# Router logits on four column tiles, copied back through another PSUM bank, and the routes of an attention-and-MoE kernel dealt to other tile steps

## The chip, the cores and the metric

The kernel runs on one core of a Trainium2 chip. The metric is the device time of one execution in microseconds, as the median of several runs. The five engines of the core have their own instruction queues, worked off in order: TensorE (PE in the profile; PEld are its weight loads), VectorE (DVE), ScalarE (ACT), GpSimd (POOL) and SyncE (SP, which here only issues DMAs).

## What is computed

Two stages, in float32. The first is a linear attention with a decaying state over 4 batches, 8 heads, 768 tokens and a head size of 48:

```python
for t in range(S):
    cur = np.einsum('bhd,bhe->bhde', u[None] * kt, vt)
    y[:, :, t] = np.einsum('bhd,bhde->bhe', rt, state + cur)
    state = w[None, :, :, None] * state + np.einsum('bhd,bhe->bhde', kt, vt)
```

The second is a mixture of experts on the 3072 token rows of 384 numbers that come out of it. A token with a positive skip score goes to the expert with its largest gate logit (8 experts, hidden size 1024), the others pass through:

```python
do_compute = x @ w_skip > 0
logits = xc @ w_gate
e_idx = np.argmax(logits, axis=1)
gate_w = probs[np.arange(len(xc)), e_idx]
y[mask] = gate_w[mask, None] * (np.maximum(xc[mask] @ w1[e], 0.0) @ w2[e])
out[do_compute] = xc + y
```

## The kernel before

**Tiles.** The tokens are cut into 24 tiles: 2 pairs of batches, 12 steps of 64 tokens, and a tile holds one step of both batches of a pair. The loop `for n in range(NT - 1)` (L905) is software-pipelined: in step n TensorE makes for tile n+1 the scores (`scores`, L441), the product with the old state (`across`, L527), for tile n+2 the transposed keys (`turn_k`, L454), for tile n the transposed output rows (`turn_x`, L569), then the new state of tile n+1 (`state`, L474) and the masked scores times values (`within`, L503). VectorE masks the scores (L462, L463) between `scores` and `within`, and prepares tile n+3 (`prep_r`, L411 and L419); GpSimd scales its keys (`prep_k`, L429) and makes half of the split of an expert weight (L114); ScalarE copies out of PSUM (`kt` L456, `xT` L572, `sblk` L483, `xt` L538) and makes the other parts of the preparation (L405, L113). `within` has an added dependence on ScalarE's copy of kt of tile n+2 (or of xT, where there is none). SP loads tile n+5, its values, and one of the first 24 weight pieces a step, and stores two output transfers for each tile (three for tiles 12 to 15).

There are 8 PSUM banks: ps_p and ps_y two each, ps_s, ps_r, ps_t, ps_l one each. Work of two engines on one bank is put in order by the builder.

**Logits.** After every fourth tile (`n % GB == GB - 1`) `gate_some` (L593) multiplies the transposed rows of four tiles with the gate and skip weights (9 columns for each of two batches, spread over a stationary side of 64 columns): 3 chunks x 2 halves = 6 matmuls of 256 moving columns into two column tiles of ps_l. ScalarE copies them to `lt` (L606). One step later `gate_back` (L608) turns them back to tokens on partitions with two matmuls against `pick` (a sum of identity columns) into the free columns of ps_t, behind the 384 columns that `turn_x` uses, and ScalarE copies them to `lg` (L621). For tiles 20 to 22 this happens at the end of the loop, and tile 23 has its own `gate` (L576).

**Routes.** `route(g0, g1)` (L634) is a generator that finds for a group of tiles each token's expert, its rank in that expert's list (with matmuls of the one-hot choice against a triangle and against ones, in ps_r), and writes token number and weight into the lists by a matmul of one-hot lanes (`ol`, L778 or L737) with values (`vl`, L789 or L744), the collect (L796 or L750). It yields a kind: 0 is VectorE work that `tick(k)` may run next, up to k pieces a step; 1, 2 and 4 mark TensorE work, run at one fixed place of a step behind `turn_x` (from step 20 on also at its end). The groups are tiles 0 to 7, 8 to 15, 16 to 19 and 20 to 23. A group can start as soon as its last logits are back. `tick` gets (1, 1, 2)[n % 3] pieces below step 16, 3 below step 20 and 6 from there on. With the group that ends at tile 15, the first gather of rows (for the first tile of expert 0, L122 on GpSimd) is issued. The first three groups run in the loop, the last behind it.

**Behind the loop** (L949 to L982) the first expert's first 128 rows are worked in pieces, `run(k)`, between the end of the attention: turn the rows, `turn_x(23)`, `gate_back` for tiles 20 to 22, three matmuls of the expert (L194), `gate(23)`, the score part of the last route, six matmuls, its rank matmuls, and so on. Then come the experts.

Of the kernel before, what the change touches and what calls it, by code (L numbers as in the profile page):

```python
# [9 lines left out]
F32 = mybir.dt.float32  # L10
F32R = mybir.dt.float32r
# [43 lines left out]
FIRST = 12  # L55
GROUPS = [(0, 8), (8, 16), (16, 20), (20, 24)]
# [3 lines left out]
def tile_wkv_moe(  # L60
# [183 lines left out]
    with ExitStack() as actx:  # L244
# [45 lines left out]
        wgp = tab.tile([P, NCC, 2, C], F32, name="wgp")  # L290
        nc.sync.dma_start(out=wgp, in_=wgq)
        pick = tab.tile([P, NB, E + 1], F32, name="pick")
# [77 lines left out]
        def setup_routes():  # L370
            nc.vector.memset(before, 0.0)
            rows = ident.rearrange("p (c q e) -> p c q e", c=2, q=NB)[:, :, :, : E + 1]
# [189 lines left out]
        gts, xcopy = {}, {}  # L562
        seen = [-1]

        def turn_x(n):
# [4 lines left out]
            if n % GB == 0:  # L570
                gts[0] = wk.tile([P, NCC, 2, GB, C], F32, tag="xT", name=f"xT{n}", bufs=1)
            xcopy[n] = nc.scalar.copy(  # L572
                gts[0][:, :, :, n % GB, :], pt[:, :DM].rearrange("p (j c t) -> p j c t", j=NCC, c=2)
            ).ins

        def gate(n):  # L576
            half = slice(n % 2 * C, (n % 2 + 1) * C)
            pg = ps_y[half, 0, DM : DM + NB * (E + 1)]
            for j in range(NCC):
                for c in range(2):  # L580
                    nc.tensor.matmul(
                        pg,
                        gts[0][:, j, c, n % GB, :],
# [9 lines left out]
        def gate_some(n, k=GB):  # L593
            pg = ps_l[:, : k * C]
            for j in range(NCC):
                for c in range(2):
                    nc.tensor.matmul(  # L597
                        pg[c * C : (c + 1) * C, :],
                        wgp[:, j, c, :],
                        gts[0][:, j, c, :k, :].rearrange("p k t -> p (k t)"),  # L600
                        start=(j == 0),
                        stop=(j == NCC - 1),
                        skip_group_check=True,
                    )
            lt = turned_lg[n] = wk.tile([P, GB * C], F32, tag="lt", name=f"lt{n}", bufs=1)[:, : k * C]
            nc.scalar.copy(lt, pg)  # L606

        def gate_back(n, k=GB):  # L608
            lt = turned_lg.pop(n)
            w = NB * (E + 1)  # L610
            for j in range(0, k, 2):
                m = min(2, k - j) * C
                nc.tensor.matmul(
                    ps_t[:m, DM + j // 2 * w : DM + (j // 2 + 1) * w],
                    lt[:, j * C : j * C + m],
                    pick.rearrange("p q e -> p (q e)"),
                    start=True,
                    stop=True,
                )
            g0, full = n - k + 1, k // 2 * 2  # L620
            nc.scalar.copy(  # L621
                lg[:, g0 : g0 + full, :].rearrange("p n e -> p (n e)"), ps_t[:, DM : DM + full // 2 * w]
            )
# [712 lines left out]
```

## Time and profile before

| | |
|---|---|
| median of 3 runs | 274.98 us (274.95 to 278.34) |
| profiled execution, its own time | 276.32 us |
| its span, first to last instruction | 274.2 us |
| busy share of the span | PE 93%, PEld 85%, DVE 67%, ACT 51%, POOL 48% |
| granted TensorE clock | 0.998 of full |
| moved by DMA | 54.30 MB, mean 198 GB/s |

A line of the profile gives start and length in us, engine, line of the kernel, operation and the tiles written and read, with xN for N merged instructions; in brackets stands the idle time before it and what ended it. A line of groups gives the busy time of all N and the mean of one in ns, then idle time and releasers. The chain is the sequence of work that ended last, each piece with what it waited for. fp32 matmuls appear as two records each.

### The profile page before, as it was taken

The page shows a single profiled execution, that of the slowest core. Times are in us where ns is not written, and L with a number is a line of the kernel's source. Part 1 is how long each engine was busy: PE and PEld are TensorE (multiplying, and loading weights), DVE is VectorE, ACT ScalarE, POOL GpSimd, SP SyncE. Part 2 cuts the span into 40 slices and gives each one's busy share as a digit, 9 for nine tenths or more (in the row PEclk, how much of TensorE's full clock was granted, in tenths as well). Part 3 has the DMA queues.
Part 4 walks back from the last instruction along what each step waited for, and adds up shares of the span by engine and source line. Part 5 has one row for each costly group of instructions (what it writes and reads, how often), then busy time and mean ns, then how long its engine had stood idle before and what let it go on. Part 6 is the DMA issues. An engine that isn't in the chain of part 4 may idle for free.

```text
span 274.2 us, 8740 instructions
## 1 busy us (share of the span) xinstructions
PE 255.6 (93%) x3545; PEld 233.9 (85%) x3545; DVE 183.2 (67%) x372; ACT 141.1 (51%) x316; POOL 131.4 (48%) x131
## 2 busy tenths in 40 slices
PE   7998999999979989788999999999999999999990
PEld 2797897878869877776879999999999999999990
DVE  8786657598896899954655686757748377483310
ACT  2664566667756756434455554717548085480300
POOL 8536313375545538511748853763525535255011
PEclk9999999999999999999999999999999999999999
DMA  7977678878999995435479994694837747100010
GB/s 201 308 197 240 163 203 277 248 247 256 289 274 282 272 284 159 114 93 143 111 254 308 365 379 166 219 317 145 260 121 241 241 142 261 43 4 27 15 35 23
DMA packets 31140, 54.30 MB, mean 198 GB/s; under 512 B 4535, under 2 KB 14412, under 8 KB 31088
## 3 DMA queue, kind: packets, MB, share of 16 engines
q1 hardware_dynamic: 28896, 48.19, 57.2%
q0 software_dynamic: 2048, 5.44, 5.8%
q8 instruction: 30, 0.49, 0.7%
q14 instruction: 22, 0.18, 0.2%
q10 hardware_dynamic: 144, 0.00, 0.0%
HBM read 45.82 MB, written 8.65 MB: 199 GB/s over the span
## 4 chain that ended last, share of the span: by engine, by line
PE 82%; DVE 10%; ACT 3%; issue 2%; DMA 1%; POOL 0%; POOLq 0%; ACTq 0%
PE ps_p L164 11%; PE ps_y L164 11%; PE ps_p L441 8%; PE ps_p L154 5%; PE ps_r L154 5%; PE ps_l L154 5%; PE ps_y L154 5%; PE ps_s L474 5%; PE ps_y L503 5%; PE ps_l L454 4%; PE ps_y L527 3%; PE ps_l L597 3%; PE ps_t L569 3%; PE ps_y L216 2%; PE ps_p L216 2%
## 5 line engine op out<-in xcount | busy, mean ns | idle before, releaser
L114 POOL TENSOR_TENSOR lo<-raw,hi 128x512 fp32r<-128x512 f32 x42 | 57.0, 1358 | 75.3 <-ACT hi L113 55.7
L113 ACT CAST hi<-raw 128x512 fp32r<-128x512 f32 x96 | 55.1, 624 | 0.0
L114 DVE TENSOR_TENSOR lo<-raw,hi 128x512 fp32r<-128x512 f32 x54 | 44.0, 837 | 2.6 <-ACT hi L113 2.3
L429 POOL TENSOR_TENSOR kd<-dm,w_d 128x512 f32<-128x512 f32 x22 | 30.1, 1366 | 14.7 <-DMA dm<-in_dm_dram 13.0
L172 POOL DMA_INDIRECT out_dram<-xg,sid x16 | 17.1, 1067 | 36.4 <-DVE xg L169 25.7
L462 DVE COPY_PREDICATED am<-below,ps_p 128x512 f32<-128x512 int8 x24 | 17.7, 739 | 17.1 <-PE ps_p L441 17.0
L441 PE MATMUL ps_p<-rd,kd 64*64 64x128 f32 x768 | 26.9, 276 | 0.3 <-issue 0.3
L441 PEld LDWEIGHTS ps_p<-rd,kd 64*64 64x64 f32 x768 | 20.9, 132 | 3.2 <-issue 0.7
L158 ACT ACTIVATE hh<-ps_p 128x464 fp32r<-128x464 f32 x7 | 3.9, 559 | 36.9 <-PE ps_p L154 20.1
L122 POOL DMA_INDIRECT xg<-out_dram,gid x16 | 18.2, 1139 | 8.7 <-DVE gw L694 4.0
L503 PE MATMUL ps_y<-vz,am 128*64 128x96 f32 x384 | 20.2, 247 | 2.1 <-DVE am L463 1.5
L503 PEld LDWEIGHTS ps_y<-vz,am 128*64 128x64 f32 x384 | 17.8, 137 | 3.4 <-issue 1.9
L405 ACT ACTIVATE rd<-rd,uw 128x128 f32<-128x128 f32 x52 | 17.8, 395 | 4.9 <-DVE rd L411 4.9
L474 PE MATMUL ps_s<-vz,kt 128*64 128x96 f32 x352 | 19.6, 253 | 0.0
L456 ACT COPY kt<-ps_l 128x512 f32<-128x512 f32 x22 | 12.8, 583 | 12.9 <-PE ps_l L454 12.9
L164 PE MATMUL ps_p<-hi,hh 128*128 128x384 f32 x56 | 19.4, 347 | 0.0
L164 PE MATMUL ps_y<-hi,hh 128*104 128x384 f32 x56 | 18.9, 338 | 0.0
L164 PE MATMUL ps_p<-hi,hl 128*128 128x384 f32 x56 | 18.9, 337 | 0.0
L164 PE MATMUL ps_y<-lo,hh 128*104 128x384 f32 x56 | 18.9, 337 | 0.0
L164 PE MATMUL ps_y<-hi,hl 128*104 128x384 f32 x56 | 18.9, 337 | 0.0
L164 PE MATMUL ps_p<-lo,hh 128*128 128x384 f32 x56 | 18.8, 336 | 0.0
L169 DVE SCALAR_TENSOR_TENSOR xg<-ps_y,gate_s,xg 104x384 f32<-104x384 f32 (+1 forms) x8 | 4.9, 616 | 20.5 <-PE ps_y L164 17.9
(244 smaller groups left out, 693.4 us busy)
## 6 DMA issues: line engine op xcount, KB each, us to landing
raw<-in_w_dram SPq DMA_DIRECT2D x96, 256.0 KB
dm<-in_dm_dram SPq DMA_DIRECT2D x24, 512.0 KB
vz<-in_tok_dram SPq DMA_DIRECT2D x48, 96.0 KB
out_dram<-xt SPq DMA_DIRECT2D x48, 96.0 KB
out_dram<-xt SPq DMA_DIRECT2D x4, 192.0 KB
xg<-out_dram,gid POOLq DMA_INDIRECT x16
out_dram<-xg,sid POOLq DMA_INDIRECT x16
wgp<-in_wgq_dram SPq DMA_DIRECT2D x1, 192.0 KB
```

The lines of the kernel that those rows point to most:

```text
L113: nc.scalar.copy(hi, t)
L114: eng.tensor_tensor(lo, t, hi.bitcast(F32), ALU.subtract)
L122: ins = nc.gpsimd.indirect_dma_start(out=xg, out_offset=None, in_=out[0:rows], in_offset=bass.IndirectOffsetOnAxis(ap=gid[:, q : q + 1], a ...
L154: nc.tensor.matmul(ph, a[:, c, fs], b[:, c, :], start=(k == 0), stop=(k == 3 * NCC - 1))
L164: nc.tensor.matmul(py, a, b[:, f, :], start=(k == 0), stop=(k == 3 * NFC - 1))
L172: ins = nc.gpsimd.indirect_dma_start(out=out, out_offset=bass.IndirectOffsetOnAxis(ap=sid[:, q : q + 1], axis=0), in_=xs.pop(q), in_offset ...
L405: nc.scalar.mul(rd[:, :, 1], rd[:, :, 0], uw[:, hp : hp + 1])
L429: (eng or nc.gpsimd).tensor_tensor(kds[n], d[:, 1], w_d[:, n % NSUB, 1][:, :, None].to_broadcast([DR, NHP, 2, C]), ALU.mult,)
L441: nc.tensor.matmul(ps_p[q * C : (q + 1) * C, a, 2 * hp * C : 2 * (hp + 1) * C], kd[h, hp, q, :], rd[h, hp, q].rearrange("p s c -> p (s c)" ...
L462: nc.vector.copy_predicated(shape(am[n % 2]), below, p[:, :, 0])
L474: nc.tensor.matmul(s[a * C : (a + 1) * C, :, hp * D : (hp + 1) * D], kt[:, hp, a, :], t[:, :, a, hp, :], start=i == 0 and hp == 0, stop=Tr ...
L503: ins = nc.tensor.matmul(place_y(a, c)[:, :, g, :], am[n % 2][:, a, hp * C : (hp + 1) * C], t[:, :, a, hp, :], start=g == 0 and n % NSTEP ...
```

## The change

- `gate_some` cuts its stationary side to 32 columns and its moving side into two halves of 128 columns (two tiles each): 12 matmuls into four column tiles of ps_l. `lt` is 128 columns wide. In the loop it is issued behind `within` and `evac` of the step, except in step 22, where it stays ahead of `within`. The call for tiles 20 to 22 takes all four places of `xT4`, the fourth with old data that nothing reads.
- `gate_back` is one matmul, with a `pick` twice as wide, into the last 36 columns of ps_r in place of ps_t.
- The transposed rows of four tiles lie in one fixed tile, `xT4`.
- The gate weights are half as large (96 KB in place of 192) and are loaded behind the loads of tile 4 in place of ahead of them.
- `tick` takes its number of pieces from the table `DEAL`; in a route of tiles 0 to 15, `ol` is a piece of its own behind `oj`. The steps at the end of steps 20 to 22 are gone. By the table the first route runs in steps 8 to 16 (its `ol` and `vl` in step 15, its collect in step 16), the second in steps 16 to 21 (`ol` and `vl` in step 20, its collect, and with it the first gather, in step 21).
- The route of tiles 16 to 19 (`mid`) no longer runs in steps 20 to 22: its score part, with the weights, runs on VectorE in step 22 behind `gate_some`, its rank matmuls, ranks, `ol` and `vl` behind the loop after `gate_back` of tiles 20 to 22, and one collect of all three values behind `gate(23)`.

```diff
+DEAL = {8: 2, 9: 2, 10: 1, 11: 1, 12: 1, 13: 1, 15: 2, 16: 4, 17: 2, 19: 2, 20: 2}
...
-        wgp = tab.tile([P, NCC, 2, C], F32, name="wgp")
-        nc.sync.dma_start(out=wgp, in_=wgq)
-        pick = tab.tile([P, NB, E + 1], F32, name="pick")
+        wgp = tab.tile([P, NCC, 2, C // 2], F32, name="wgp")
+        pick = tab.tile([P, 2, NB, E + 1], F32, name="pick")
...
         def gate_some(n, k=GB):
-            pg = ps_l[:, : k * C]
+            pg = ps_l[:, : 2 * C]
+            w = C // 2
             for j in range(NCC):
                 for c in range(2):
-                    nc.tensor.matmul(
-                        pg[c * C : (c + 1) * C, :],
-                        wgp[:, j, c, :],
-                        gts[0][:, j, c, :k, :].rearrange("p k t -> p (k t)"),
...
+                    for i in range(2):
+                        nc.tensor.matmul(
+                            pg[(2 * c + i) * w : (2 * c + i + 1) * w, :],
+                            wgp[:, j, c, :],
+                            xT4[:, j, c, 2 * i : 2 * i + 2, :].rearrange("p k t -> p (k t)"),
...
         def gate_back(n, k=GB):
             lt = turned_lg.pop(n)
             w = NB * (E + 1)
-            for j in range(0, k, 2):
-                m = min(2, k - j) * C
-                nc.tensor.matmul(
-                    ps_t[:m, DM + j // 2 * w : DM + (j // 2 + 1) * w],
-                    lt[:, j * C : j * C + m],
-                    pick.rearrange("p q e -> p (q e)"),
...
+            pb = ps_r[:, 512 - 2 * w :]
+            nc.tensor.matmul(pb, lt, pick.rearrange("p s q e -> p (s q e)"), start=True, stop=True)
             g0, full = n - k + 1, k // 2 * 2
-            nc.scalar.copy(
-                lg[:, g0 : g0 + full, :].rearrange("p n e -> p (n e)"), ps_t[:, DM : DM + full // 2 * w]
-            )
+            nc.scalar.copy(lg[:, g0 : g0 + full, :].rearrange("p n e -> p (n e)"), pb[:, : full // 2 * w])
...
         def route(g0, g1):
-            n, late = g1 - g0, g0 >= EARLY
+            n, late, mid = g1 - g0, g0 >= EARLY, EARLY <= g0 and g1 < NT
...
+            if mid:
+                weigh()
+                part_weight()
+                count()
             yield 4 if late else 1
...
                 value(0)
+                if mid:
+                    value(1, 2)
+                    nc.vector.tensor_tensor(before, before, sums, ALU.add)
+                    nc.vector.tensor_scalar(over[:, g0:g1], r1, float(CAP), None, ALU.is_ge)
+                    yield 4
+                    collect(0, NV3)
+                    return
...
-            nc.vector.tensor_tensor(
-                ol, lane[:, None, :].to_broadcast([P, n, P]), lo.unsqueeze(2).to_broadcast([P, n, P]), ALU.is_equal
-            )
             oj = small("oj", w=NSL)
...
             nc.vector.tensor_tensor(before, before, sums, ALU.add)
+            yield 0
+            nc.vector.tensor_tensor(
+                ol, lane[:, None, :].to_broadcast([P, n, P]), lo.unsqueeze(2).to_broadcast([P, n, P]), ALU.is_equal
+            )
             yield 0
...
         load_v(4)
+        nc.sync.dma_start(out=wgp, in_=wgq)
...
-            tick((1, 1, 2)[n % 3] if n < EARLY else 3 if n < TE else 6)
+            tick(DEAL.get(n, 0))
...
+            if n == NT - 2:
+                gate_some(n, NT - 1 - TE)
+                while next(mid) == 0:
+                    pass
+            within(n + 1, kcopy.get(n + 2, xcopy[n]))
+            evac(n + 1)
             if n < TE and n % GB == GB - 1:
                 gate_some(n)
-            elif n == NT - 2:
-                gate_some(n, NT - 1 - TE)
-            within(n + 1, kcopy.get(n + 2, xcopy[n]))
-            evac(n + 1)
             if back:
                 back()
-            if n >= TE:
-                for kind in (1, 2, 4):
-                    step_route(kind)
-                tick()
...
         gate_back(NT - 2, NT - 1 - TE)
+        while next(mid) == 0:
+            pass
         run(1)
         gate(NT - 1)
-        last = route(ends[NT], NT)
+        both(mid)
+        last = route(*GROUPS[3])
```

More of the change, by code (lines that the diff above doesn't have):

```diff
@@ L371, in setup_routes @@
             nc.vector.memset(before, 0.0)
-            rows = ident.rearrange("p (c q e) -> p c q e", c=2, q=NB)[:, :, :, : E + 1]
+            rows = ident.rearrange("p (c s q e) -> p c s q e", c=2, s=2, q=NB)[:, :, :, :, : E + 1]
             nc.vector.tensor_tensor(pick, rows[:, 0], rows[:, 1], ALU.add)
@@ L560, in put_x @@
                 x_out.append(ins.ins)
-        gts, xcopy = {}, {}
+        xT4 = tab.tile([P, NCC, 2, GB, C], F32, name="xT4")
+        xcopy = {}
         seen = [-1]
@@ L569, in turn_x @@
                 nc.tensor.transpose(pt[:, c * P : (c + 1) * P], x[:, c * P : (c + 1) * P], ident)
[L570 to L571 removed]
             xcopy[n] = nc.scalar.copy(
[L573 removed]
+                xT4[:, :, :, n % GB, :], pt[:, :DM].rearrange("p (j c t) -> p j c t", j=NCC, c=2)
             ).ins
@@ L662, in route @@
             yield 0
-            if not late:
+            if not late or mid:
                 nc.scalar.activation(df, df, AF.Exp)
@@ L670, in route, with weigh, part_weight, count @@
             nc.vector.tensor_tensor(oh, eq[:, :, :E], bc(m2), ALU.is_equal)
+            gw = small("gw")
+            gh, gl = small("gh", F32R), small("gl", F32R)
+            sums = sm.tile([P, E], F32, tag="sums", name=f"sums{g0}")
+            def weigh():
+                nc.vector.tensor_reduce(gw, df, AX.X, ALU.add)
+                nc.vector.tensor_scalar(gw, gw, 1e-9, None, ALU.add)
+            def part_weight():
+                nc.vector.reciprocal(gw, gw)
+                nc.vector.tensor_copy(gh, gw)
+                nc.vector.tensor_tensor(gl, gw, gh.bitcast(F32), ALU.subtract)
+            def count():
+                nc.vector.tensor_reduce(sums, oh.rearrange("p n e -> p e n"), AX.X, ALU.add)
+            if mid:
+                weigh()
+                part_weight()
+                count()
             yield 4 if late else 1
@@ L690, in route @@
                 )
-            gw = small("gw")
-            def weigh():
-                nc.vector.tensor_reduce(gw, df, AX.X, ALU.add)
-                nc.vector.tensor_scalar(gw, gw, 1e-9, None, ALU.add)
-            if late:
+            if late and not mid:
                 nc.scalar.activation(df, df, AF.Exp)
-            else:
+            elif not late:
                 weigh()
@@ L702, in route @@
             rk = small("rkp", w=E)
-            gh, gl = small("gh", F32R), small("gl", F32R)
             r1 = small("r1")
-            sums = sm.tile([P, E], F32, tag="sums", name=f"sums{g0}")
             def ranks():
                 nc.vector.tensor_tensor(rk, pr[:, : n * E].rearrange("p (n e) -> p n e", e=E), oh, ALU.mult)
-            def count():
-                nc.vector.tensor_reduce(sums, oh.rearrange("p n e -> p e n"), AX.X, ALU.add)
             if late:
@@ L819, in place @@
             nc.vector.tensor_tensor(gate_s[:, c], lists[:, 1, j], lists[:, 2, j], ALU.add)
-        ends = {g1: g0 for g0, g1 in GROUPS}
+        ends = {g1: g0 for g0, g1 in GROUPS if g1 <= EARLY}
+        mid = route(*GROUPS[2])
         routes = []
@@ L948, in tile_wkv_moe @@
                 piece(n - FIRST_LOAD)
+        assert not routes
         done = NT - 1 - FIRST_LOAD - LEAD
```

32 lines of the change are left out of this document (11 added, 21 removed).

## The prediction, made before the changed kernel ran

> **What bounds the kernel now.** I read the page's head and its chain first, then the chain of waits step by step, then the groups, then the engine timelines of VectorE and TensorE where the chain leaves TensorE.
>
> ```profile
> span 274.2 us, 8740 instructions
> DMA  7977678878999995435479994694837747100010
> PE 82%; DVE 10%; ACT 3%; issue 2%; DMA 1%; POOL 0%; POOLq 0%; ACTq 0%
> ```
>
> 82% of the chain is TensorE; the 10% of VectorE stand at a few places of the attention, which ends shortly before 124.98 us, where the first expert's matmuls begin (a row of part 4). The experts behind it are nearly one run of TensorE, and the change doesn't touch them. So I count what the change does to TensorE's time up to the end of the last attention tile, and then in the bridge to the experts. One undisturbed tile step on the chain:
>
> ```profile
> 35.41 1.03 PE ps_p L441 x32
> 36.44 0.45 PE ps_y L527 x32
> 36.89 0.59 PE ps_l L454 x4
> 37.48 0.33 PE ps_t L569 x3
> 37.81 0.81 PE ps_s L474 x16
> 38.62 0.66 PE ps_y L503 x16
> ```
>
> Scores, across, turn_k, turn_x, state, within: 3.87 us with no gap. Everything a step has above 3.87 is what the change can win.
>
> **Part 1, logits on four column tiles.** Now a call of gate_some is 6 fp32 matmuls (12 records) of 256 columns on two column tiles; then 12 matmuls (24 records) of 128 columns on four.
>
> ```profile
> L597 PE MATMUL ps_l<-xT,wgp 128*64 128x256 f32 x60 | 7.5, 382 | 0.0
> L597 PEld LDWEIGHTS ps_l<-xT,wgp 128*64 128x64 f32 x72 | 5.1, 136 | 2.2 <-ACT xT L572 0.8
> L441 PE MATMUL ps_p<-rd,kd 64*64 64x128 f32 x768 | 26.9, 276 | 0.3 <-issue 0.3
> ```
>
> Five calls take 7.5 us: 1.5 us each, 125 ns a record on two tiles. No record here has a 128x32 tile. The nearest is L441: four tiles at once, 128 columns, 26.9 / 768 = 35 ns a record, and its one change of tile shape per call is in that rate. 24 x 35 ns = 0.84 us. Bounds: if the records scale with columns and tiles alone, 125 / 4 = 31 ns, 0.75 us; if only two of four tiles run at a time, 62.5 ns, 1.5 us and no gain. I take 0.84: saving 0.66 x 5 = 3.3 us. The sixth call (three tiles, 192 columns, by its columns about 1.1 us now; afterwards the same as the others) saves 0.3. Sum **-3.6 us** (-4.1 to +0.4).
>
> The order changes too: state, within and the old gate all use 128x64 tiles, the new gate doesn't, so one more change of shape comes in. The quoted step shows what that may cost: the 16 records of state, behind 128x128 work, take 0.81 us, the same 16 of within, behind state, 0.66: 0.15 us, less than the spread of my bounds. The Trainium skill (TensorEngine Tiling (Array Packing), Key Properties) says against this change that switching the tiling mode, not merely the tile, drains TensorE; it names no price. With 0.15 us a call from the rows above the sum would be 0.75 us less over five calls; I hold it to be in L441's rate already. The same page gives up to 4x for a stationary side of 32 columns, which no run here shows yet.
>
> Putting the gate behind within and evac costs nothing: ScalarE's copy of the logits comes behind the tile's evacuation, ahead of the next turn_k by scores and across (1.48 us); without that cover turn_k would wait for a copy that is smaller than kt's 0.59 us. Loading the weights of the gate (half as large) behind tile 4's loads puts its issue (0.33 us of SP, below) from ahead of tile 4's load to behind the first tile's two output transfers and tile 4's, and ahead of tile 5's load; the first call that reads it comes three steps later, and tile 5 is needed a step later than tile 4.
>
> ```profile
> 9.19 0.33 SPq L291 DMA_DIRECT2D wgp<-in_wgq_dram  x1
> ```
>
> **Part 2, brought back into another bank.** Every fourth step, turn_x writes ps_t, where gate_back has just left logits for ScalarE:
>
> ```profile
> 32.04 0.60 PE ps_l L454 x4
> 32.66 0.59 ACT kt L456
> 33.39 0.55 PE ps_t L569 x3
> PE ps_t L569 <- ACT lg L621: 2.1, 5, 0.5
> L613 PE MATMUL ps_t<-pick,lt 128*128 128x18 f32 x20 | 2.6, 244 | 0.0
> ```
>
> From 32.64 to 33.94 for what takes 0.33 in the quiet step: 0.97 us lost, five times. The transposes start where the lg copy ends, which sits behind the kt copy. With the logits in ps_r that wait has no object; what stays is one matmul in place of two, at most 2.6 / 5 / 2 = 0.26 us. Saving 0.71 x 5 = **-3.6 us** (-4.8 if even the matmul hides in the queue, -1.3 if the wait stays for another reason and only matmuls go). But ps_r is the bank of the routes: at step 16 the collect of the first route, now at step 15, comes right behind gate_back and waits for the same copy, **+0.2 us**.
>
> **Part 3, the table of steps.** VectorE per tile step:
>
> ```profile
> L462 DVE COPY_PREDICATED am<-below,ps_p 128x512 f32<-128x512 int8 x24 | 17.7, 739 | 17.1 <-PE ps_p L441 17.0
> L463 DVE COPY_PREDICATED am<-eye,ps_p 128x512 f32<-128x512 int8 x24 | 17.7, 736 | 0.9
> L411 DVE TENSOR_TENSOR rd<-dm,w_d 128x512 f32<-128x512 f32 x24 | 18.2, 759 | 0.0
> L419 DVE TENSOR_TENSOR rd<-rd,uw 128x256 f32<-128x256 f32 x22 | 13.5, 614 | 0.6
> L778 DVE TENSOR_TENSOR ol<-lane,lo 128x1024 fp32r<-128x1024 f32 x2 | 4.1, 2042 | 0.0
> 79.65 0.28 DVE L789 TENSOR_TENSOR vl<-oj,id 128x128 fp32r<-128x128 f32 x1
> L695 DVE TENSOR_SCALAR gw<-gw 128x8 f32<-128x8 f32 x2 | 1.9, 961 | 0.1
> 79.90 0.88 PE L503 MATMUL ps_y<-vz,am 128*64 128x96 f32 x16 [1.52 <-DVE am L463]
> 101.77 0.81 PE L527 MATMUL ps_y<-sblk,rd 64*64 64x48 f32 x32 [1.17 <-DVE sblk L486]
> ```
>
> Mask and preparation are 2.85 us, so 1.0 us of a 3.87 us step is free for a route, and TensorE tolerates another 0.7 (2.18 us from the end of scores to within, less 1.48 of masking). Before, ol (2.04) falls into step 13, a bare step, and within waits 1.52; steps 17 and 18 push VectorE so far that across waits 1.17 and then runs 0.36 longer. The table puts ol and the three vl writes (0.28 each, 2.9 in all) into steps 15 and 20, and nothing into 14 and 18. Step 15 is followed by a gate (0.84) and the longer step 16, so 2.9 - 1.0 - 0.84 = 1.1 us of delay falls on a step with 1.2 us or more of extra TensorE work: no wait. So -1.52 and -1.53, **-3.1 us**. Step 20 has no such cover: 2.9 - 1.0 - 0.26 = 1.6 us late in step 21, which has no turn_k but takes the collect of the second route (1.05, below): it tolerates 1.1. A wait of 0.5 there, 0.2 in step 11 (two route pieces fell to step 10), 0.2 in steps 17 to 20: **+0.9 us** (0 to 3: L695 takes 961 ns for 8 numbers a partition, so a small piece can stand most of a microsecond beside other work, and three such pieces in steps 10, 17 and 20 make the upper end).
>
> **Part 4, tiles 16 to 19 behind the attention.** In steps 20 to 22 this route now holds TensorE three times:
>
> ```profile
> 109.66 1.05 PE L796 MATMUL ps_r<-vl,ol 128*128 128x48 f32 x8
> 112.58 0.18 PE L673 MATMUL ps_r<-oh,tri 128*128 128x32 bf16 x1 [0.40 <-DVE oh L670]
> 115.86 0.61 PE L750 MATMUL ps_r<-vl,ol 128*128 128x8 f32 x4 [1.06 <-DVE vl L744]
> 118.45 0.61 PE L750 MATMUL ps_r<-vl,ol 128*128 128x16 f32 x4 [0.20 <-DVE vl L744]
> ```
>
> Waits 0.40 + 1.06 + 0.20 and work 0.2 + 0.6 + 0.6: **-3.1 us** there. It comes back in the bridge:
>
> ```profile
> 124.98 0.90 PE ps_p L194 x3
> 125.62 0.17 ACT L625 COPY lg<-ps_t 64x18 f32<-64x18 f32 x1
> 125.88 0.80 PE ps_y L581 x12
> 126.68 1.59 PE ps_p L194 x6
> 128.43 0.20 DVE rkp L708
> 129.56 0.12 DVE vl L744
> 129.72 0.62 PE ps_l L750 x4
> ```
>
> The rank matmuls of the middle route write ps_r, so they wait for the lg copies, which end at 125.79, and TensorE takes its instructions in order: the first expert's three matmuls (124.98), the gate of tile 23 and all behind them wait 0.85 us more, and 0.2 of rank matmuls. While TensorE does 0.9 + 0.8, VectorE ranks and spreads (rkp to vl 1.25 above, two more vl 0.24), just in time; then one collect of 0.6 stands ahead of the six matmuls at 126.68, and mx waits behind its lists write. Sum **+1.7 us** (0.6 without the wait for lg, 2.2 if VectorE is late too). The score work of this route, gone into step 22, is 13 small pieces, 2.6 us at rkp's 0.2; beside them stand the gate, within and the turning of the first expert's rows (0.84 + 0.66 + about 1), which VectorE otherwise spends idle. What isn't covered, 0.1 us, would come on the first expert.
>
> The first gather is issued a step later:
>
> ```profile
> 111.46 1.26 POOL L122 DMA_INDIRECT xg<-out_dram,gid  x1 [1.15 <-DVE em L817]
> q0 software_dynamic: 37, 0.08, 40.0%
> ```
>
> Its last packets move between 114.0 and 114.5 (second row): 3.3 us from the row numbers to landing. From the row numbers in step 21 to the end of within(23) I count within 0.66, scores 1.03, across 0.45, turn_x 0.33, its copy 0.5 (shorter than kt's 0.59), gate 0.84, within 0.66, less 0.4 for the lists: 4.1 us. It is covered, by 0.8 us only.
>
> **Sum.** -3.6 - 3.6 + 0.2 - 3.1 + 0.9 - 3.1 + 1.7 = -10.6 us. The profiled execution took 276.32 us (274.2 span and 2.1 around it), 1.3 above the median of 274.98. Its span would be 263.6 and its time 265.7; the median, with the same gain, **264.4 us**.
>
> **Rivals.**
> *Two of four column tiles at a time* (1.5 us a call): +4 us, 268.4. For it: no record of a 128x32 tile. Against: four 64x64 tiles do overlap.
> *The transfers become the bound.* Slices 5 to 14 of the DMA row (34 to 103 us) show 7 to 9 tenths; I take away 7 of these 68.5 us. At a mean share of 0.9 the bytes need 61.7 us: nothing left over, and late tiles would give back about 2.5: 266.9. Against: loads run two steps ahead.
> *The wait of turn_x isn't for the bank* but for ScalarE's order, and stays: 3.6 shrinks to 1.3, 266.7. So the change wouldn't do what it says. Against: it appears in five of five gate_back steps and in no other.
> *VectorE takes the gain back* (upper ends of parts 3 and 4: 2.1 + 0.5): 267.0.
> *Slower:* the 32-wide tiles don't overlap at all and each load stands open: 125 ns and 136 ns of weight load (L597's rows) for each record make 6.3 us a call, 5.4 more than I count, six times: 297 us. It decides from 0.84 + 10.6 / 6 = 2.6 us a call, 108 ns a record. Against: at 64x64, L441's 35 ns is far below its own 276 ns.
>
> **Chances.** Forecast 0.66, two at a time 0.10, transfers 0.08, wait stays 0.05, VectorE 0.08, slower 0.03. The range holds the first five and the unknown costs: the best ends of all parts together are 264.4 - 0.5 - 1.2 - 0.9 - 1.1 = 260.7, and two tiles at a time with the upper end of part 3 are 268.4 + 2.1 = 270.5. Two per cent (5.5 us) is about what a measurement of this kernel can tell from no change; below 269.5 lie nearly all cases: faster 0.88, same 0.09, slower 0.03.
>
> **What would show it.** L597 in 24 records a call of about 0.85 us; no wait of L569 for lg; no wait over 1 us of within for am at step 14 or of across for sblk at step 19; one at within(22) below 1 us; the first expert's L194 near 113.5 us (124.98 less 12.3 of the loop, plus 0.85 of its new wait); in the bridge L673 waiting for lg and the last route's L648 some 1.7 us later behind within(23) than now. Wrong if a 24-record call is over 1.3 us, if L569 still waits, or if steps 12 to 20 show TensorE or GpSimd waiting for dm.

## The result: 0.987 of the time before, and the profile after

| | before | after |
|---|---|---|
| median | 275.9 us (274.95 to 278.34, 4 runs) | 273.88 us (271.42 to 274.71, 4 runs) |
| ratio | | 0.9874, 95% interval 0.9828 to 0.9921 |
| profiled execution: time, span | 276.32, 274.2 us | 274.71, 273.0 us |

Forecast were 264.4 us, in a range from 260.7 to 270.5. Of the 10.6 us, 2.0 came by the medians and 3.5 by the ratio; the time lies outside the range, and the gain, 0.8 to 1.7%, stays below the two per cent that the prediction held to be about the least that can be told from no change. The ratios, here and below, set executions aside that count as slow, so they can differ from the quotient of the medians.

The head of the page after, its DMA slices and its chain by engine:

```profile
span 273.0 us, 8866 instructions
...
DMA  6978668889799898543589994685847647001010
...
PE 78%; DMA 6%; DVE 5%; issue 3%; ACT 3%; SPq 2%; POOL 1%; POOLq 0%; DVEq 0%
```

The chain went over TensorE for 82% of the span and over DMA for 1%; now DMA and SP's queue have 8%. VectorE fell from 10% to 5%: its waits went, as intended. Others came.

**The changed places themselves.** One step with gate and gate_back in the chain after:

```profile
30.23 0.79 PE ps_l L598 x24
...
32.50 0.59 PE ps_l L454 x4
33.09 0.15 PE ps_r L613 x2
33.24 0.36 PE ps_t L570 x3
33.59 0.38 issue
```

The gate takes 0.79 us (0.84 forecast), gate_back 0.15, and `turn_x` (L570) follows turn_k without a wait. The last row is another matter: "issue" is a gap of TensorE for which the profile names no cause; the last part comes back to it.

The waits of TensorE between 9 and 125 us (line, what it waited for: sum, times, longest):

```profile
PE ps_y L503 <- ACT kt L456: 2.0, 2, 1.3
PE ps_r L798 <- ACT lg L615: 1.7, 1, 1.7
PE ps_y L527 <- issue: 1.3, 2, 1.1
PE ps_r L684 <- ACT lg L617: 1.1, 1, 1.1
PE ps_l L454 <- ACT kt L456: 1.1, 1, 1.1
...
PE ps_y L503 <- DVE lists L803: 0.7, 1, 0.7
PE ps_r L798 <- DVE vl L791: 0.6, 1, 0.6
```

No wait for the mask `am` or for `sblk` is left. In their place TensorE waits for ScalarE's kt (3.1 us, 0.8 before) and lg. ScalarE was late because it works in order and stood in front of a weight piece that had not landed (L114 splits `raw`; no such wait before):

```profile
ACT hi L114 <- DMA raw<-in_w_dram: 5.8, 4, 2.1
```

**Where the time went, by stage.** I cut the span at the start of within(0), (5), (19), (23) and at the first matmul of the first expert's second half. These are the rows of TensorE's timeline, before:

```profile
11.38 0.83 PE L503 MATMUL ps_y<-vz,am 128*64 128x96 f32 x16
34.58 0.67 PE L503 MATMUL ps_y<-vz,am 128*64 128x96 f32 x12
98.74 0.83 PE L503 MATMUL ps_y<-vz,am 128*64 128x96 f32 x16
122.62 0.58 PE L503 MATMUL ps_y<-vz,am 128*64 128x96 f32 x10
138.19 0.51 PE L194 MATMUL ps_l<-hi,xhl 128*128 128x512 f32 x1
```

and after:

```profile
12.01 0.67 PE L503 MATMUL ps_y<-vz,am 128*64 128x96 f32 x12
34.63 0.58 PE L503 MATMUL ps_y<-vz,am 128*64 128x96 f32 x9
98.98 0.75 PE L503 MATMUL ps_y<-vz,am 128*64 128x96 f32 x14
119.12 0.47 PE L503 MATMUL ps_y<-vz,am 128*64 128x96 f32 x6
136.44 0.50 PE L195 MATMUL ps_l<-hi,xhl 128*128 128x512 f32 x1
```

| stage | before | after | difference | forecast (its terms by step) |
|---|---|---|---|---|
| to within(0) | 11.4 | 12.0 | +0.6 | 0 |
| within(0) to (5) | 23.2 | 22.6 | -0.6 | -1.4 |
| within(5) to (19) | 64.2 | 64.3 | +0.2 | -6.6 |
| within(19) to (23) | 23.9 | 20.1 | -3.7 | -4.3 |
| bridge | 15.6 | 17.3 | +1.75 | +1.7 |
| rest | 136.0 | 136.6 | +0.6 | 0 |

The forecast column sorts the prediction's own terms by where they fall: a gate 0.66 and a gate_back 0.71 ahead of within(5); three of each and 3.1 of part 3, less 0.6 of new waits, from (5) to (19); then 0.66 + 0.71 + 0.3 + 3.1 - 0.5. Most of the miss, 6.8 of 9.4 us, lies in one stage: between within(5) and within(19) the change won nothing.

### The profile page after: what moved, and what is told of

Its sections match the earlier page's. It is cut to its first block, busy times and chain, and to the rows that moved or that the text cites. A ratio compares the mean times of both kernels' runs of the same rounds, so it can differ in the third digit from the quotient of the medians.

```text
span 273.0 us, 8866 instructions
## 1 busy us (share of the span) xinstructions
PE 251.9 (92%) x3600; PEld 229.9 (84%) x3601; DVE 182.9 (67%) x371; ACT 139.9 (51%) x316; POOL 130.6 (48%) x131
## 4 chain that ended last, share of the span: by engine, by line
PE 78%; DMA 6%; DVE 5%; issue 3%; ACT 3%; SPq 2%; POOL 1%; POOLq 0%; DVEq 0%
PE ps_p L165 11%; PE ps_y L165 11%; PE ps_p L441 7%; PE ps_y L503 5%; PE ps_p L155 5%; PE ps_r L155 5%; PE ps_l L155 5%; PE ps_s L474 5%; PE ps_y L155 5%; PE ps_l L454 4%; PE ps_y L527 3%; DMA vz<-in_tok_dram 2%; DMA dm<-in_dm_dram 2%; PE ps_t L570 2%; DMA raw<-in_w_dram 2%
## 5 line engine op out<-in xcount | busy, mean ns | idle before, releaser
L115 POOL TENSOR_TENSOR lo<-raw,hi 128x512 fp32r<-128x512 f32 x42 | 56.3, 1340 | 69.6 <-ACT hi L114 63.7
L114 ACT CAST hi<-raw 128x512 fp32r<-128x512 f32 x96 | 55.1, 624 | 5.8 <-DMA raw<-in_w_dram 5.8
L429 POOL TENSOR_TENSOR kd<-dm,w_d 128x512 f32<-128x512 f32 x22 | 30.2, 1373 | 15.9 <-DMA dm<-in_dm_dram 14.2
L411 DVE TENSOR_TENSOR rd<-dm,w_d 128x512 f32<-128x512 f32 x24 | 19.9, 830 | 2.8 <-DMA dm<-in_dm_dram 2.8
L503 PEld LDWEIGHTS ps_y<-vz,am 128*64 128x64 f32 x384 | 17.3, 137 | 4.3 <-ACT kt L456 2.6
L165 PE MATMUL ps_p<-hi,hh 128*128 128x384 f32 x56 | 19.4, 347 | 0.0
L165 PE MATMUL ps_y<-hi,hh 128*104 128x384 f32 x56 | 18.9, 338 | 0.0
L165 PE MATMUL ps_p<-hi,hl 128*128 128x384 f32 x56 | 18.9, 337 | 0.0
L165 PE MATMUL ps_y<-lo,hh 128*104 128x384 f32 x56 | 18.9, 337 | 0.0
L165 PE MATMUL ps_y<-hi,hl 128*104 128x384 f32 x56 | 18.9, 337 | 0.0
L474 PEld LDWEIGHTS ps_s<-vz,kt 128*64 128x64 f32 x352 | 15.5, 136 | 4.0 <-issue 3.1
```

Of the source, the lines that this page charges most:

```text
L114: nc.scalar.copy(hi, t)
L115: eng.tensor_tensor(lo, t, hi.bitcast(F32), ALU.subtract)
L165: nc.tensor.matmul(py, a, b[:, f, :], start=(k == 0), stop=(k == 3 * NFC - 1))
L411: nc.vector.tensor_tensor(rds[n][:, :, :, 0], d[:, 0], w_d[:, n % NSUB, 0][:, :, None].to_broadcast([DR, NHP, 2, C]), ALU.mult,)
L429: (eng or nc.gpsimd).tensor_tensor(kds[n], d[:, 1], w_d[:, n % NSUB, 1][:, :, None].to_broadcast([DR, NHP, 2, C]), ALU.mult,)
L474: nc.tensor.matmul(s[a * C : (a + 1) * C, :, hp * D : (hp + 1) * D], kt[:, hp, a, :], t[:, :, a, hp, :], start=i == 0 and hp == 0, stop=Tr ...
```

## What the experiments showed

The experiments ran in five groups, on four chips, each group with the kernel before beside it (its median 276.9, 277.8, 276.8, 275.7 and 275.9 us in turn); across groups only the ratios can be compared. Stage lengths of each profiled execution, in us, read as above; "half clock" is how long TensorE's granted clock stood at 0.5 before the last stage. The last column is the ratio to before.

| run | 0-5 | 5-19 | 19-23 | bridge | half clock | median us | ratio, 95% interval |
|---|---|---|---|---|---|---|---|
| e10_before | 23.1 | 64.3 | 27.0 | 16.3 | 10.2 | 279.96 (one run) | |
| e6_after | 20.3 | 63.6 | 19.1 | 20.7 | 10.2 | 273.06 | 0.9845, 0.9788 to 0.9903 |
| e1_third_later | 20.3 | 62.6 | 19.1 | 22.0 | 13.7 | 273.44 | 0.9890, 0.9821 to 0.9959 |
| e3_split_late | 20.3 | 66.1 | 18.4 | 18.7 | 3.4 | 272.64 | 0.9831, 0.9760 to 0.9902 |
| e4_back_ps_t | 20.7 | 62.7 | 18.4 | 18.4 | 3.4 | 271.42 | 0.9833, 0.9756 to 0.9910 |
| e5_raw_two | 20.3 | 70.5 | 18.9 | 18.6 | 10.2 | 278.24 | 1.0056, 1.0016 to 1.0097 |
| e7_bridge | 20.3 | 61.6 | 18.5 | 17.0 | 0 | 271.34 | 0.9803, 0.9749 to 0.9857 |
| e8_bridge_third | 20.3 | 62.2 | 19.2 | 17.0 | 0 | 267.87 | 0.9633, 0.9572 to 0.9693 |
| e9_third_warm | 20.7 | 61.0 | 19.4 | 17.3 | 0 | 268.85 | 0.9716, 0.9654 to 0.9778 |
| e11_warm | 20.3 | 65.1 | 21.7 | 17.3 | 3.4 | 272.92 | 0.9876, 0.9819 to 0.9934 |
| e12_parts12 | 20.3 | 63.2 | 26.3 | 15.4 | 10.2 | 274.94 | 0.9960, 0.9926 to 0.9995 |
| e13_old_table | 20.3 | 62.6 | 22.9 | 17.3 | 3.4 | 275.23 | 0.9835, 0.9728 to 0.9941 |

### First: is it the number of transfers, or ScalarE's order?

The theory after the first profile (T): weight pieces land late, ScalarE waits for them ahead of kt, TensorE waits for kt. e1_third_later takes the third output transfer of tiles 12 to 15 out of these steps:

```diff
-            if FIRST <= n < EARLY:
-                r0 = (B - NB) * S + (EARLY - NSTEP) * C + (n - FIRST) * P
-                put_x(out[r0 : r0 + P, :], x, True)
+            if n in (19, 20):
+                r0 = (B - NB) * S + (21 - NSTEP) * C + (n - 19) * 96
+                put_x(out[r0 : r0 + 96, :], x[:96], True)
```

> The changed kernel, with the third output transfers of tiles 12 to 15 (192 KB each, which only fill rows before the first gather) taken out of steps 11 to 14; two smaller ones (144 KB, for the rows that are still unwritten then) stand beside tiles 19 and 20. Theory T (SP's transfers bound steps 11 to 16 once TensorE is faster): the raw waits of ScalarE, 5.8 us in all, fall below 2; within(13) to within(17), 22.0 us in the changed kernel, falls to about 18.5; time about 270.5 against 273.9. Rival V (the new table of route steps costs VectorE and TensorE what the gate gave): those steps stay at 22 us, time 273.5 to 274.

e3_split_late puts ScalarE's split of a piece behind the copies that TensorE needs (`piece(..., split=True)` moved behind `prep_k`):

> The changed kernel, with the split of the expert weight piece (ScalarE's cast L114, which waits for the raw piece) moved behind turn_x and prep_k in each step, so that it no longer stands ahead of ScalarE's kt and lg copies. Theory T1 (a late raw piece hurts only through ScalarE's order): TensorE's waits for kt in steps 14 and 15 (0.70 and 1.28 us) and for lg in step 16 (1.7 us) vanish, time about 271. Theory T2 (the transfers themselves are too slow there): the wait shows up elsewhere, at dm or at the output rows, and the time stays within 1 us of 273.9. Rival V: no change either, but with the waits for kt unchanged.

e4_back_ps_t sends the last gate_back into ps_t, so that the rank matmuls of the bridge don't wait for lg:

```diff
-            pb = ps_r[:, 512 - 2 * w :]
+            pb = (ps_t if n == NT - 2 else ps_r)[:, 512 - 2 * w :]
```

> The changed kernel, with the last gate_back alone (tiles 20 to 22, behind the loop) writing ps_t, which nothing else uses there. If the rank matmuls of the middle route wait in the bridge only because their bank is being copied out, the wait of 1.07 us at L684 falls below 0.3 and the time is about 1 us less, 272.9. If VectorE's ranks set the bridge anyway: no wait for lg, but within 0.3 us of the same time.

e5_raw_two loads each of the 19 pieces of the loop in two transfers of half the columns:

> The changed kernel, with each raw weight piece of the attention loop loaded by two transfers of 128 KB in place of one of 256: the same bytes, 19 more transfers. If the number of transfers is what binds (SP's issue of about 0.55 us each, and the eight that can be under way, since each waits for the eighth before it), steps 11 to 17 get some 4 us longer and the time is 277 or more. If bytes bind: within 1 us of 273.9. Rival V: within 1 us too.

One more transfer a step costs time: within(5) to (19) took 70.5 us (6.8 of them at half clock), and the median is some 5 us above what the changed kernel gives beside the same before (0.987 of 276.9 is 273.3). The other three moved the time little, and two of the traces showed why: within(23) of e1_third_later started at 113.4 us, 5.7 earlier than in the first profile, and its bridge took 22.0 us in place of 17.3. The waits for pieces are gone in e1, as theory T asked, but within(13) to within(17) took 20.1 us, not 18.5, and the second execution of the unchanged kernel below has no such wait either, so this sign proves nothing for T. In e4 the wait for lg at L684 is gone too; in its place TensorE waits 1.1 us for VectorE's `vl`, and its time can't be told from that of the changed kernel. Late splits (e3) only moved the wait: TensorE then waited 2.3 us for the mask and 1.2 for a value of the route.

### Second: the clock in the bridge

In e1_third_later the matmuls of the bridge were slower; the windows show the clock (the column PEclk, third from the end):

```profile
113.40:117.90 4.50, 3.32 (x39) 2.42 (x37) 2.57 (x12) 2.48 (x8) 1.28 (x1) 1.00 0.59 140
117.90:131.30 13.40, 13.40 (x55) 11.11 (x54) 6.19 (x34) 2.70 (x8) 4.30 (x4) 0.50 0.32 99
```

For these 13.4 us (13.7 in all, from 118.0 to 131.6) TensorE ran at half clock, right behind a stretch in which it waited for the logits, 1.07 us, and for ScalarE's xt before it. Theory G: such idle time in the bridge halves the clock. A second execution of the unchanged kernel:

> The changed kernel once more, unchanged, beside the kernel before: a second profile. Theory A (the gain of the loop is taken by stalls that differ from execution to execution: transfers that land late, gaps of TensorE inside a group): within(23) starts somewhere between 113 and 119 us (119.1 in the first profile), and the median is 0.985 to 0.99 of before, some 273 us. Theory B (the first profile shows the kernel as it always runs): within(23) starts at 119 again, to within 0.5 us.

e7_bridge is e4_back_ps_t with the collect of the middle route moved between the first expert's matmuls:

```diff
         run(1)
         gate(NT - 1)
+        run(1)
         both(mid)
         last = route(*GROUPS[3])
         while next(last) == 0:
             pass
-        run(2)
+        run(1)
```

> The last gate_back writes ps_t, and the collect of the middle route stands between the first and the second three of the expert's six matmuls, so TensorE has work while VectorE makes ol and vl. Theory G (the granted TensorE clock is halved when TensorE stands idle for much of a few us, as it does in the bridge): no halved clock between 110 and 140 us, and the bridge from within(23) to the first expert's second half is 15.5 to 16 us in place of 17.3: about 2 us faster than the changed kernel, 271. Rival H (the clock falls for a reason of its own, whatever TensorE does in the bridge): the clock is at 0.5 for 3 us or more again, and the kernel is within 1 us of the changed one.

e8_bridge_third is that together with e1_third_later:

> The bridge as in e7_bridge, and the third output transfers of tiles 12 to 15 put behind tiles 19 and 20 as in e1_third_later. Theory T+G (SP's queue holds the loop back, and idle time in the bridge costs the clock): within(23) starts near 113.4 us as in e1_third_later, the bridge takes 15.5 to 16 us at full clock, the rest 136.3: span 265.5, time 267.5. If the clock is halved all the same (H): 4 to 5 us more, 272. If the early end of the loop in e1_third_later was chance (the transfers aren't what holds it): within(23) at 115 to 117, time 270 to 271.

e9_third_warm is e1_third_later with `warm(5)`, five matmuls without a use, behind the last gate_back:

> e1_third_later with five matmuls of no use (bf16 ones, 128x512, into ps_t, which nothing reads then) in the place where TensorE waits 1.07 us for the logits of tiles 16 to 22. They depend on nothing that is late and take about 1.1 us at full clock. Theory G (idle time halves the clock): the clock stays at 1.00 from 115 to 135 us, the bridge takes 17.3 us in place of 22.0, and the time is 4 us below e1_third_later, 269. Rival H (another cause): the clock is at 0.5 for 10 us or more again, time 273 or, with the matmuls on top, 274.

e6_after ended its loop at 114.4 us and then ran 10.2 us at half clock; the first profile had its loop at 119.1 and full clock. So theory A holds: the stalls differ from execution to execution, and the second profile is no better than the first, by another way. e9_third_warm:

```profile
112.50:117.00 4.50, 4.39 (x46) 2.83 (x41) 2.56 (x12) 2.48 (x8) 1.28 (x1) 1.00 0.57 136
117.00:130.00 13.00, 11.88 (x80) 9.96 (x79) 7.89 (x37) 4.46 (x12) 6.19 (x6) 1.00 0.42 126
```

TensorE is busy 4.39 of the first 4.50 us, where e1_third_later had 3.32; the clock stays, the bridge takes 17.3 us, and the median is 268.85 beside 273.44: 0.9716 against 0.9890 of before. Rival H, by which the clock falls whatever TensorE does, is refuted by the times, whose intervals lie apart: the added work only fills idle time. e8_bridge_third came to 267.87 where 267.5 was expected; it beats the kernel before and the changed one. It also beats e7_bridge of the same group, with intervals apart (0.9572 to 0.9693 and 0.9749 to 0.9857), so moving four output transfers is worth 1.7% by the ratios, 1.3% by the medians, once the clock doesn't take it back. My size for e7's bridge was off: 17.0 us, not 15.5 to 16. The idle time there is VectorE's chain from the ranks to the values (0.25, 0.48, 0.53 and 0.38 us of waits in e8), short enough to keep the clock.

### Third: the parts, and the kernel before

> The kernel before, unchanged, for a second profile beside the others. If the executions of before differ as those of the changed kernel do: within(23) starts between 119 and 125 us (122.6 in the first profile), the bridge from there to the first expert's second half takes 15.6 us again, at full clock, since TensorE hardly idles in it; time 275 to 278. If the clock is halved in before as well, the bridge takes 17 to 20 us.

> The changed kernel with five matmuls of no use (bf16 ones, 128x512, into ps_t) where TensorE waits 1.07 us for the logits; nothing else. Theory G (the idle stretch there halves the clock in most executions): clock 1.00 from 110 to 135 us, bridge 17.3 us, time 269.5 to 270.5, that is 3 us below the 273.06 of the changed kernel. Rival (the halved clock is a matter of the loop's end, and the third transfers were needed too): 272.5 to 273.5.

e12_parts12 is the kernel before with the gate, gate_back, `wgp`, `pick` and `xT4` of the change, the gate called behind `evac`; table, routes and bridge are old:

> The kernel before with parts 1 and 2 alone: four column tiles behind within, and gate_back into ps_r; the table, the routes and the bridge are those of before. By the prediction's terms for these parts -3.6 - 3.6 = -7.2 us: 270.5 beside 277.8 of before, with the bridge of before at full clock. If the loop gives gains of TensorE back to late transfers (as the first profile showed, 4.2 of 12): -4.7, 273. If nothing of it arrives: within 1 us of before.

e13_old_table differs from the changed kernel in one line:

```diff
-            tick(DEAL.get(n, 0))
+            tick((1, 1, 2)[n % 3] if n < EARLY else 3)
```

> The changed kernel with the number of pieces of before (1, 1, 2 in turn, 3 from step 16 on) in place of the table; routes, bridge and gate as changed. By the prediction's part 3 the table is worth 3.1 - 0.9 = 2.2 us: 275.3 beside the 273.06 of the changed kernel, with within at step 13 or 14 and across near step 18 waiting over 1 us for VectorE. If the table is worth nothing, because another wait stands behind the one it removes: 272.5 to 273.5.

e10_before repeats the stages of before to within 0.2 us up to within(19), and then it too fell to half clock, 10.2 us long, behind its wait of 1.05 us for `vl` ahead of within(22). So the kernel before has that loss in some executions; my expectation, that its bridge keeps the clock, looked at the wrong place. e11_warm kept full clock in the bridge (17.3 us) as G says, yet its 272.92 us lie where the rival had put them: its loop ended at 118.3 us, with ScalarE waiting 13.6 us in all for pieces and 3.4 us of half clock in step 21. Filling the bridge alone didn't pay here.

In e12_parts12 parts 1 and 2 are 2.9 us ahead of the first profile of before at within(5) (1.0 of them a gap without a releaser that before has there) and another 1.0 at within(19), and give 2.4 of it back behind that, where gate_back in step 20 now shares ps_r with the second route:

```profile
107.48 0.17 PE L784 MATMUL ps_r<-before,ones 128*128 128x8 bf16 x1 [3.03 <-ACT lg L614]
```

3.03 us of wait, and 6.8 us at half clock around it. The forecast had +0.2 us for this bank, at step 16. Over its runs e12_parts12 is 0.4% below before, about 1 us of the 7.2. The old table in the changed kernel (e13) brings back 3.5 us of waits of `across` for `sblk`. Its ratio to before stays where it was, 0.9835 against 0.9845, with the interval 2% wide; its median, 275.23 us, is what the 2.2 us of part 3 would give, but its six times lie between 269.63 and 281.9. What the table is worth is neither shown nor excluded.

### Fourth: SP's queue or the amount of data?

e14_act_out issues the stores of the attention rows on ScalarE's queue (`nc.scalar.dma_start` in `put_x`); e16_bridge_act and e15_best do it in e7_bridge and e8_bridge_third.

> The changed kernel with the stores of the attention rows (2 to 3 a tile) issued from ScalarE's queue in place of SP's; same data, same number. Theory Q (SP's queue makes loads late): ScalarE's waits for raw vanish, within(23) starts at 112 to 114 us, and the time falls by up to 2 us to 271 (the clock of the bridge takes a part, as in e1_third_later). Theory D (the amount of data is the limit: 1.15 MB a step, 1.34 MB in steps 12 to 15, at the 265 to 295 GB/s seen): raw waits as before, within(23) at 114 to 119, time 273, or 1 to 2 us more for 1.1 us of issuing a step on ScalarE.

> e7_bridge with the stores on ScalarE's queue. Theory Q: as e8_bridge_third without moving the third transfers, 268, and a narrow spread. Theory D: as e7_bridge, 271.3 with a spread of some 6 us, or 1 to 2 us more.

> e8_bridge_third with the stores on ScalarE's queue: bridge filled, third transfers moved, stores off SP. Theory Q: the loop loses its last late loads too, within(23) at 111.5 to 112.5 us, time 266.5. Theory D: the third transfers were what was too much, the rest fits: 267.9 as e8_bridge_third, or 1 us more for ScalarE's issuing.

Neither theory: 289.59, 287.08 and 284.93 us, ratios 1.0383 (1.0326 to 1.0441), 1.0371 (1.0327 to 1.0415), 1.0305 (1.0264 to 1.0347). ScalarE's timeline of e14_act_out:

```profile
59.87 1.53 ACTq L556 DMA_DIRECT2D out_dram<-xt  x2
61.45 0.62 ACT L114 CAST hi<-raw 128x512 fp32r<-128x512 f32 x1 [1.61 <-issue]
...
64.63 2.47 ACTq L556 DMA_DIRECT2D out_dram<-xt  x2
```

Two issues hold ScalarE for 1.53 us, and its round is 4.76 us (59.87 to 64.63) without any late piece. TensorE waited 10.1 us for its kt in this loop, so ScalarE had become the bound, and these runs don't tell the theories apart. The next three do it by size: pieces 4 to 18 are loaded by half, in the same number of transfers, into four fixed tiles.

```diff
-        t = raw[e, j] = pool.tile([P, QC], F32, tag="raw", name=f"raw{e}_{j}", bufs=bufs)
+            t = raw[e, j] = rawfix[k % NST]
+            w = QC // 2 if NST <= k < 19 else QC
...
-        nc.sync.dma_start(out=t, in_=w12[e, :, j * QC : (j + 1) * QC])
+        nc.sync.dma_start(out=t[:, :w], in_=w12[e, :, j * QC : j * QC + w])
```

> e7_bridge with raw pieces 4 to 18 loaded by half (256 of 512 columns, 128 KB in place of 256; the other half keeps an older piece, so these parts of the weights of the first two experts are wrong; the number of transfers and all arithmetic stay). Theory D (the amount of data holds the loop: 1.15 MB a step becomes 1.02): no waits of ScalarE for raw, within(23) at 111 to 113 us in nearly every execution, time 267 to 268 with a narrow spread. Theory Q (the number of transfers on SP's queue): as e7_bridge, 271.3 with a spread of 6 us.

> e8_bridge_third with the raw pieces 4 to 18 loaded by half as in e17_bridge_half_raw. Theory D: if data still holds e8_bridge_third in steps 12 to 15, 266 to 267; if moving the third transfers was enough, 267.9 as there. Theory Q: 267.9.

> The kernel before with raw pieces 4 to 18 loaded by half. If data holds the loop only at the pace of the changed kernel: within 1 us of before. If it held the kernel before as well: 2 us or more below it, and the gain of the change that was predicted would have been partly data already in before.

The times (277.12, 275.00 and 283.36 us; ratios 1.0005, 0.9940, 1.0284) can't be read: with fixed tiles, piece 20 is loaded into the tile of piece 16, whose split comes later in the program and now waits for that load, and the bridges took 22.1, 22.9 and 21.8 us. The stage from within(5) to (19) lies ahead of that. It took 62.3, 65.7 (with 6.8 at half clock) and 64.7 us, beside 61.6, 62.2 and 64.2 of the kernels that they are made from, and ScalarE still waited for pieces in e17:

```profile
ACT hi L121 <- DMA raw<-in_w_dram: 4.9, 6, 1.6
```

Half the data of a piece didn't shorten the loop. That speaks against theory D, but no more: each is one profile, and the fixed tiles also change what a load has to wait for.

## Why the prediction was wrong, step by step

**Part 1: right.** 24 records take 0.79 us, 33 ns each; 0.84 was forecast, and the four tiles work at once. The rivals of two at a time (1.5 us) and of none (6.3 us) are out.

**Part 2: right where it was aimed, mis-sized beside.** The five waits of `turn_x` are gone and gate_back takes 0.15 us. But +0.2 us for sharing ps_r with the routes was 1.7 in the first profile (L798), 1.1 in e7_bridge, none in e6_after, and 3.03 in e12_parts12: it is as long as ScalarE is late with lg.

**Part 3: the waits went, the time didn't come.** Waits for `am` and `sblk` are gone; the new ones for VectorE are 0.7 + 0.6 us where +0.9 was forecast, though the writes of `vl`, counted as 0.28 us each, took 1.36 in four of six cases of the first profile. That removing the old waits was worth 2.2 us isn't shown by e13_old_table.

**Part 4: right, but for the clock.** The stage that holds steps 20 to 22 won 3.7 us in the first profile and 4.8 in the second, where all terms that fall into it came to 4.3; the bridge cost 1.75 us, of which TensorE's timeline shows

```profile
122.36 0.18 PE L684 MATMUL ps_r<-oh,tri 128*128 128x32 bf16 x1 [1.07 <-ACT lg L617]
```

1.07 us where 0.85 was forecast.

**The step that failed.** It stands at the start of the prediction: "Everything a step has above 3.87 is what the change can win." It doesn't hold for steps 5 to 18: from within(5) to within(19) 57.6 us were forecast, and the two profiles of the changed kernel took 64.3 and 63.6. The rival that would have said so, "The transfers become the bound", was put off with "Against: loads run two steps ahead" and priced at 2.5 us from the mean share of the DMA engines. The sign that the prediction had named for it came in the first profile: between 70 and 109 us GpSimd waited 1.1 us for dm and VectorE 2.0, where before neither did. (In the second profile neither does.) SP's own timeline, of which the prediction read a single row, was in the profile of before:

```profile
61.24 0.54 SPq L108 DMA_DIRECT2D raw<-in_w_dram  x1
61.89 0.37 SPq L271 DMA_DIRECT2D dm<-in_dm_dram  x1
62.35 1.85 SPq L279 DMA_DIRECT2D vz<-in_tok_dram  x2
64.30 1.35 SPq L556 DMA_DIRECT2D out_dram<-xt  x2
65.74 0.54 SPq L108 DMA_DIRECT2D raw<-in_w_dram  x1
...
68.12 2.83 SPq L556 DMA_DIRECT2D out_dram<-xt  x3
71.05 0.54 SPq L108 DMA_DIRECT2D raw<-in_w_dram  x1
```

and after:

```profile
61.09 0.55 SPq L109 DMA_DIRECT2D raw<-in_w_dram  x1
...
65.89 0.54 SPq L109 DMA_DIRECT2D raw<-in_w_dram  x1
66.54 1.26 SPq L272 DMA_DIRECT2D dm<-in_dm_dram  x1
67.89 1.16 SPq L280 DMA_DIRECT2D vz<-in_tok_dram  x2
69.14 1.93 SPq L556 DMA_DIRECT2D out_dram<-xt  x3
71.17 2.31 SPq L109 DMA_DIRECT2D raw<-in_w_dram  x1
```

One issue follows the other with 0.1 us between. At their usual lengths a round is 0.54 + 0.37 + 1.16 + 1.35 us and four gaps of 0.1: 3.8 us, and 4.4 with the third store. The forecast needed 57.6 us for 14 steps, 4.1 a step; 10 such rounds and 4 longer ones are already 56, and some issues are longer (1.85, 2.31 and 2.83 in the rows above). For the 13 rounds from piece 0 to piece 13 SP took 60.4 and 63.3 us in the two profiles of before, 62.6 and 61.7 in the two of the changed kernel: 4.6 to 4.9 us a round, of which 7 to 9 us in all are what the long issues take beyond their usual length. So the pace of SP stayed what it was, and both kernels issue pieces 5 to 7 within 0.2 us of the same moment, 61.1 to 71.2 us from the start. What TensorE saved came off the distance between a load and its use. Before, pieces 0 to 12 were split 4.6 to 8.0 us after their issue, without a wait; after, pieces 7 to 9 (the issue at 71.17 is piece 7) 4.3 to 5.0 us after it, as soon as they land, and ScalarE waits:

```profile
75.91 0.62 ACT L114 CAST hi<-raw 128x512 fp32r<-128x512 f32 x1 [1.64 <-DMA raw<-in_w_dram]
81.61 0.62 ACT L114 CAST hi<-raw 128x512 fp32r<-128x512 f32 x1 [1.58 <-DMA raw<-in_w_dram]
87.49 0.62 ACT L114 CAST hi<-raw 128x512 fp32r<-128x512 f32 x1 [2.13 <-DMA raw<-in_w_dram]
```

Why some issues are long can be read from the traces, though not by the names that the profile gives. Between the loads run transfers that bring the engines' instructions, 16 KB each (`q8 instruction` in the DMA view). In e6_after one of them runs from 71.82 to 72.88 us, and the issue of a piece takes 1.55 us instead of 0.55 (first SP's timeline, then the DMA view from 71.8 to 72.9 us):

```profile
71.71 1.55 SPq L109 DMA_DIRECT2D raw<-in_w_dram  x1
q8 instruction: 1, 0.02, 6.0%
```

It ends 0.38 us behind that transfer. In the profiles of the table and the first ones of before and after, 14 in all, 239 of the 243 issues of SP over 0.85 us between within(1) and within(23) hold the end of such a transfer, and 220 end 0.33 to 0.43 us behind it; of the 1512 shorter issues only 23 hold one. That the two go together is shown so; how one delays the other is not.

And late pieces aren't all of it. In the stage from within(5) to (19) TensorE is busy for 59.3 us in the first profile and 59.2 in e6_after. In the first it waits 3.7 us for kt and lg. e6_after has no wait for a piece; its 63.6 us hold five gaps of TensorE inside groups of its own, 3.6 us in all, without a releaser:

```profile
68.71 0.54 PE L441 MATMUL ps_p<-rd,kd 64*64 64x128 f32 x10 [0.55 <-issue]
74.24 0.55 PE L527 MATMUL ps_y<-sblk,rd 64*64 64x48 f32 x19 [0.80 <-issue]
80.14 0.44 PE L570 MATMUL ps_t<-ident,xt 128*128 128x128 f32 x2 [0.79 <-issue]
```

They look like late instructions: the gaps end 1.2 to 1.4 us behind an instruction transfer (74.24 behind the one that ended at 72.88), and of the 38 such gaps in the same 14 profiles 37 end 1.2 to 1.65 us behind one. No run here changed the instructions to test it.

What was shown: one transfer more a step is dear (e5: 70.5 us for the stage), and four less pay when the clock allows it (e8 against e7). What stays open is how the 6.8 us divide: two executions that lose their time in different places come out 0.7 us apart, which fits a pace that SP sets, but no run took the long issues away, and e17 doesn't show that less data wouldn't help.

**What no step had: the clock.** The bridge cost +1.7 us as forecast, but TensorE's clock was also halved there in e1, e3, e4, e5 and e6, five of the seven profiles that have the idle stretch, and in none of the four where it is filled (e7, e8, e9, e11). That cost 3.3 us in e6_after (20.7 less 17.3) and 4.6 in e1_third_later. The Trainium skill (TensorE: Matmul & The Clock Gate, Part 1) says that the clock falls to half after an idle window of about 3.4 us and comes back after a busy one. The traces agree on the half and on the unit: the stretches are 3.4, 6.8, 10.2 and 13.7 us long. They don't need 3.4 us of idling: 1.0 to 2.1 us of idle time in the 3.4 us ahead were enough in the runs of the table (1.2 in e1 and e6), and 13.7 us of full work had to pass in e1 until the clock was back. Nor is every such stretch punished:

```profile
80.00:90.00 10.00, 7.01 (x166) 6.00 (x158) 8.13 (x11) 5.38 (x15) 5.11 (x5) 1.00 0.93 274
```

Here, in the first profile of the changed kernel, TensorE idled 3 us of 10, 1.7 of them within 3.4 us, and kept its clock. What decides between the two is open.

## What to carry to other kernels

Before a wait of the busiest engine is counted as gain, lay the timeline of the queue that feeds it beside the forecast: if its round of issues, the long ones counted in, is as long as the step you hope for, the wait only moves to the data. Price an idle stretch of TensorE with the clock that may follow it, and put independent matmuls there, even useless ones; two fixes that measured nothing alone (0.989 and 0.988 of before, beside 0.985 without them) came to 0.972 together (e1, e11, e9). Where executions of one kernel differ by 3 us in the place where they lose time, look at two profiles before explaining one.

## What was not expected of the hardware

- Four 128x32 column tiles in fp32 run at 33 ns a record of 128 columns, as four 64x64 tiles do.
- At half clock three of the expert's 512-column records take 1.48 us (e1_third_later) in place of 0.85 at full clock.
- An issue of a transfer holds ScalarE for 0.76 us, where SP needs 0.37 to 0.65.
- An issue of SP that falls together with a transfer of instructions takes on average 0.7 to 0.8 us longer (before, after and e6_after), and gaps of TensorE without a releaser end 1.2 to 1.65 us behind such a transfer.
- A write of `vl` takes VectorE 0.28 or 1.36 us: in e6_after the one beside GpSimd's L429 (79.94 to 82.20 us) takes 1.36, and the two behind it 0.28. The three of the second route took 2.77 us in the first profile after, with GpSimd at work from 107.1 to 112.1 us:

```profile
109.46 2.77 DVE vl L791 x3
```
